# Softmax sums of eight head pairs moved from GpSimd to TensorE, later due times for weight, block and tap writes, and score banks lent to the dense layers, in an attention, gated-convolution and channel-mix kernel

## The chip, the cores and the metric

The program runs on one core of one Trainium2 chip. The time is device microseconds from one launch; lower is better. The core has a matrix engine (TensorE, PE in the rows), three engines for element-wise work (VectorE or DVE, ScalarE or ACT, GpSimd or POOL), and a queue engine (SyncE, SP) that issues all DMAs here. Results of matmuls land in PSUM banks.

## The reference

For 4 batches, 12 heads, 448 rows and 64 columns per head:

```
scores = cap * tanh(q k^T / sqrt(64) / cap)
attn   = exp(scores - max) / (sum(exp(scores - max)) + 1e-9)
x      = attn v, heads side by side: 4 x 448 x 768
gate   = sigmoid(sum over 5 taps of conv_w[k] * x shifted by k rows)
x      = (gate * (x w_val)) w_out
xk, xr = mixtures of x and x shifted by one row, with mu_k and mu_r
out    = sigmoid(xr w_r) * ((max(xk w_k, 0))^2 w_v)
```

q, k and v are 32-bit floats. The weights arrive as 64-bit floats, which the kernel reads as pairs of 32-bit words and narrows itself. w_val, w_out and w_r are 768 x 768, w_k 768 x 1024, w_v 1024 x 768.

## The kernel before, in words

Everything is kept transposed, features on the partitions, 448 rows in the free dimension. Two heads make a pair; there are 24 pairs, six to a batch. A dense product takes each operand as two parts, `hi` (a rounded copy) and `lo` (the rest), and multiplies hi by hi, hi by lo and lo by hi, so one 128 x 128 block costs three matmuls (L644).

**A pair** is six pieces (`piece`, L720). Piece 0: scores of key blocks 0 and 1, tanh on ScalarE (L246), exp on ScalarE (L253), and the first add of the exps on GpSimd (`add_up`, L262). Piece 1: the product with v of the pair before (`pv`, L286), and its copy to `x_f` on ScalarE (L288). Pieces 2 and 3: the transposes of the next pair's q and k on TensorE (L211), split on VectorE (L172, L175) or later ScalarE and VectorE. Piece 4: key blocks 2 and 3, tanh, exp, the other adds (L271, L274). Piece 5: `sums` of the pair before: two matmuls with a block of ones over the added-up exps (L294), which give each row's sum on all 64 partitions of its head. For the last two pairs of a batch VectorE turns the sums into reciprocals at once (L299, L300); for the others the sums go through DRAM and come back as R. `prep` then has GpSimd multiply `x_f` by R (L379), splits it into the block's parts (`x_split`), and adds up the five taps of the gate (L390 on ScalarE for the first, L396 on VectorE for the others). A sigmoid over the whole gate (L400) ends it.

**Order.** The order on every engine is the order of the program text: `in_order` ties each instruction to the one before it on its engine, so an instruction that waits holds all behind it. Work is put later by `post(n, ...)`, which runs it n calls of `step()` from now; a step is one piece, or one half of a dense output.

**Stages.** The first eight pairs (`FIRST`, L20) run by themselves, with the narrowing of the first three w_val blocks between them (L456 to L461). Then the dense layers val and out run batch by batch (`first_stage`), with the rest of the pairs put between their halves at 1.5, 1.5 and 1.35 pieces a half (`behind_first`, L794). In batch 0 each weight block of val and out is narrowed one block ahead and cut into parts by `w_make` (L492): hi on ScalarE, lo on GpSimd or VectorE, the result stored to DRAM for the other batches. The narrowed block lies in one of two buffers (`mk`, L114), so a new block's first step (L456, ScalarE) waits until both halves' lo parts of the block two before are made. With batch 3 the attention is over; w_k and w_v are narrowed into resident tiles while val, out and the second stage (r, k, v; `second_stage`) run. `evac` (L567) takes each dense result out of PSUM; `store` (L612) transposes each output block on TensorE and sends it out.

**PSUM.** `ps_d` has two banks for dense results, `ps_s` two tiles of two banks each for scores, `ps_v` and `ps_m` one each.

The lines that the change touches: `add_up` (L262), `pv` (L276), `sums` (L290), the due times in `prep` (L403 to L412), `x_split` (L426), `w_make` (L492), and the PSUM tile and the place of `store` in `layer` (L625).

Of the kernel before, what the change touches and what calls it, by code (L numbers as in the profile page):

```python
# [46 lines left out]
def attention_gated_conv_channel_mix_kernel(  # L47
# [78 lines left out]
    ones = const.tile([128, 64], F32, name="ones")  # L126
    inv_c = const.tile([128, 1], F32, name="inv_c")
# [13 lines left out]
    def dma(**kw):  # L141
        nc.sync.dma_start(**kw)
# [119 lines left out]
    def add_up(i, n):  # L262

        t = t_t[i]
        eng = nc.gpsimd
        if n == 0:
            acc_t[i] = pools["x"].tile([128, 2, S], F32, tag="acc", name="acc")
            eng.tensor_tensor(acc_t[i], t[:, 0:2], t[:, 2:4], ALU.add)  # L268
            return
        acc = acc_t[i]  # L270
        eng.tensor_tensor(acc, acc, t[:, 4:6], ALU.add)  # L271
        for h in range(2):
            r = slice(64 * h, 64 * h + 64)
            eng.tensor_tensor(acc[r, h], acc[r, h], t[r, 6], ALU.add)  # L274

    def pv(i):  # L276
# [4 lines left out]
        t = t_t.pop(i)  # L281
# [8 lines left out]
    def sums(i):  # L290
        acc = acc_t.pop(i)
        ps = ps_m.tile([128, S], F32, tag="sum", name="sum")
        for h in range(2):
            nc.tensor.matmul(ps[64 * h:64 * h + 64], lhsT=ones, rhs=acc[:, h], start=True, stop=True)  # L294
# [74 lines left out]
    def prep(b, hp, early=False):  # L369
# [39 lines left out]
        for k in range(TAPS):  # L409
            at(4 + (k + 1) // 2 if early else 15 + k, tap, k)  # L410
        if hp == KD - 1:
            at(4 + (TAPS + 1) // 2 if early else 15 + TAPS, sigmoid)  # L412
# [13 lines left out]
    def x_split(b, hp):  # L426
        assert again[0] or b * NP + hp in divided
        x_blk[b, hp] = split_blk(x_f[b * NP + hp], nc.scalar, engines["PD"[hp % 2]], 0 if again[0] else 1)
# [63 lines left out]
    def w_make(nm, o, a, lo_eng):  # L492
# [4 lines left out]
        split_hi(nc.scalar, wp[:, 0], t)  # L497
        post(2 if steps[0] < dense_from[0] else 1, split_lo, lo_eng, wp[:, 1], t, wp[:, 0])
        post(7, lambda: dma(out=parts_d[nm, o][a], in_=wp.bitcast(F32)))
# [122 lines left out]
    n_half = [-1]  # L622
    pend = []

    def layer(b, nm, behind):  # L625
# [4 lines left out]
        for o in range(no):  # L630
            ps = ps_d.tile([128, S], F32, tag="d", name="psd")
            for a in range(2):
# [3 lines left out]
                for kk in range(a * h, a * h + h):  # L636
# [11 lines left out]
                    if kk == 1 and pend:  # L648
                        store(*pend.pop())
# [56 lines left out]
    nc.vector.memset(ones, 1.0)  # L706
    for n in range(2):
        for h in range(2):
            nc.gpsimd.memset(vz[n][h][64 - 64 * h:128 - 64 * h], 0.0)
# [148 lines left out]
    def end_first():  # L858
# [5 lines left out]
        w_resident()  # L864

# [12 lines left out]
    with tc.If(cap_bits > CAP_BITS):  # L878
# [4 lines left out]
        again[0] = True  # L883
        stage.enter_context(first_pools())
# [47 lines left out]
```

## Time and profile before

| | us |
|---|---|
| three runs | 859.79, 860.77, 861.51 (median 860.77) |
| the profiled execution, its own time | 858.22 |
| its span, first to last instruction | 856.4 |
| TensorE busy in the span | 752.1 (88%) |
| VectorE busy | 496.3 (58%) |
| ScalarE busy | 441.9 (52%) |
| GpSimd busy | 344.7 (40%) |
| mean granted TensorE clock, of full speed | 0.952 |

The busy times are of engines that run side by side, so they do not add up to the span, and each is an average over stages with different limits. The row "PEclk" of the profile and of its windows is the granted clock of TensorE as a share of full speed, 2.4 GHz; it has two levels, 2.4 and 1.2 GHz, and a value between is a mean over a stretch. In rows of a timeline the first number is the start, the second the duration in microseconds, and the bracket gives the idle time of the engine before the instruction and what ended it. An "x2" matmul of the program shows as two or four records where the profiler cuts 32-bit matmuls in two, and a few records are missing.

### The profile page before, as it was taken

The numbers are of one execution on the slowest core, as the hardware profiler recorded it, in microseconds if no ns is written. First come the engines' busy times: TensorE is split into PE (matmuls) and PEld (weight loads), VectorE is DVE, ScalarE is ACT, GpSimd is POOL, SyncE is SP. The second block draws the span as 40 slices with busy tenths as digits, with TensorE's granted clock in tenths as the row PEclk, the third lists the DMA queues.
The fourth block names the chain that finished last, engine by engine and source line by source line (L and its number), as shares of the span: only waits on it lengthen the run. The fifth ranks groups of instructions, "written<-read, shape, count | busy, mean of one in ns | idle before, by whom it ended". The sixth has DMA issues, their size and how long they took to land.

```text
span 856.4 us, 10628 instructions
## 1 busy us (share of the span) xinstructions
PE 752.1 (88%) x3798; PEld 578.8 (68%) x3798; DVE 496.3 (58%) x646; ACT 441.9 (52%) x669; POOL 344.7 (40%) x262
## 2 busy tenths in 40 slices
PE   5986678886889798899979887979999999999996
PEld 3433345554556455576668777769999999999996
DVE  5579968968737677654477676885323332333320
ACT  5775566565577566756443465443433353335310
POOL 3787645657535466545716557781000000000000
PEclk8899789988999999999999999999999999999999
DMA  5633316667556677664577996332901380244001
GB/s 140 181 87 99 95 49 192 196 195 220 159 173 203 209 239 230 192 182 134 173 248 242 320 325 227 97 119 73 290 11 43 108 265 1 57 136 149 1 22 47
DMA packets 143931, 131.23 MB, mean 153 GB/s; under 512 B 75767, under 2 KB 123895, under 8 KB 143870
## 3 DMA queue, kind: packets, MB, share of 16 engines
q1 hardware_dynamic: 143870, 130.47, 50.0%
q8 instruction: 32, 0.52, 0.3%
q14 instruction: 29, 0.24, 0.1%
HBM read 105.16 MB, written 25.22 MB: 152 GB/s over the span
## 4 chain that ended last, share of the span: by engine, by line
PE 44%; DVE 23%; ACT 12%; DMA 8%; POOL 7%; issue 5%; SPq 1%; POOLq 0%; ACTq 0%; DVEq 0%
PE psd L644 37%; DVE gate L396 7%; DVE wr L460 3%; PE pv L286 3%; PE s L244 2%; ACT t L253 2%; ACT t L246 2%; DVE wr L459 2%; DMA of<-out 2%; POOL acc L271 2%; DVE wr L461 2%; POOL acc L274 2%; DMA x<-in_moe_w_k_dram 1%; POOL xf L379 1%; ACT t L249 1%
## 5 line engine op out<-in xcount | busy, mean ns | idle before, releaser
L644 PE MATMUL psd<-blk,wp 128*128 128x448 f32 x1296 | 298.5, 383 | 26.1 <-DVE blk L175 9.9
L644 PEld LDWEIGHTS psd<-blk,wp 128*128 128x128 f32 x1296 | 246.5, 196 | 73.5 <-issue 21.5
L644 PE MATMUL psd<-blk,wv 128*128 128x448 f32 x576 | 125.8, 375 | 1.4 <-ACT blk L170 1.1
L644 PE MATMUL psd<-blk,wk 128*128 128x448 f32 x576 | 118.5, 366 | 2.7 <-DVE f L589 2.6
L644 PEld LDWEIGHTS psd<-blk,wk 128*128 128x128 f32 x576 | 107.9, 188 | 12.7 <-DVE f L589 4.2
L644 PEld LDWEIGHTS psd<-blk,wv 128*128 128x128 f32 x576 | 109.0, 192 | 10.8 <-ACT blk L170 1.5
L170 ACT CAST blk<-f 128x448 fp32r<-128x448 f32 x104 | 58.9, 567 | 105.0 <-DVE f L605 51.4
L396 DVE SCALAR_TENSOR_TENSOR gate<-xf,vecT,gate 128x447 f32<-128x447 f32 (+2 forms) x96 | 88.7, 936 | 33.2 <-ACT gate L390 32.3
L175 DVE TENSOR_TENSOR blk<-f,blk 128x448 fp32r<-128x448 f32 x104 | 77.4, 744 | 49.4 <-ACT blk L170 49.4
L271 POOL TENSOR_TENSOR acc<-acc,t 128x896 f32<-128x896 f32 x24 | 52.5, 2189 | 108.3 <-ACT t L253 108.2
L244 PE MATMUL s<-qh,kh 64*128 64x448 f32 x192 | 45.1, 463 | 39.1 <-ACT t L246 24.8
L253 ACT ACTIVATE t<-t 128x1792 f32<-128x1792 f32 (+1 forms) x48 | 72.6, 1512 | 1.5
L246 ACT ACTIVATE t<-s 128x896 f32<-128x896 f32 x72 | 63.7, 915 | 17.3 <-PE s L244 17.2
L286 PE MATMUL pv<-t,vn 128*64 128x448 f32 x288 | 67.1, 606 | 0.0
L274 POOL TENSOR_TENSOR acc<-acc,t 64x448 f32<-64x448 f32 x48 | 62.5, 1303 | 3.6
L268 POOL TENSOR_TENSOR acc<-t 128x896 f32<-128x896 f32 x24 | 54.0, 2248 | 22.5 <-ACT t L253 13.5
L605 DVE SCALAR_TENSOR_TENSOR f<-of,vecT,prev 128x448 f32<-128x448 f32 x48 | 33.5, 698 | 48.0 <-ACT prev L603 48.0
L244 PEld LDWEIGHTS s<-qh,kh 64*128 64x128 f32 x192 | 18.7, 188 | 61.8 <-ACT t L246 35.3
L458 POOL TENSOR_SCALAR wr<-wr 128x384 f32<-128x384 f32 (+1 forms) x28 | 53.8, 1921 | 15.9 <-ACT wr L456 15.8
L589 DVE TENSOR_TENSOR f<-psd,kr 128x448 f32<-128x448 f32 x32 | 19.9, 622 | 61.4 <-ACT kr L587 61.4
L460 DVE SCALAR_TENSOR_TENSOR wr<-x,wr 128x768 int32<-128x768 int32 (+2 forms) x46 | 49.3, 1072 | 1.6
L618 ACT COPY on<-pso 112x512 f32<-112x512 f32 x24 | 14.1, 586 | 68.1 <-PE pso L616 67.8
(81 smaller groups left out, 911.2 us busy)
## 6 DMA issues: line engine op xcount, KB each, us to landing
wp<-pdr SPq DMA_DIRECT2D x48, 384.0 KB
wp<-pdval SPq DMA_DIRECT2D x36, 384.0 KB
wp<-pdout SPq DMA_DIRECT2D x36, 384.0 KB
of<-out SPq DMA_DIRECT2D x48, 224.0 KB
x<-in_moe_w_k_dram SPq DMA_DIRECT2D x16, 384.0 KB
x<-in_moe_w_v_dram SPq DMA_DIRECT2D x12, 512.0 KB
qn<-in_q_dram SPq DMA_DIRECT2D x48, 112.0 KB
kn<-in_k_dram SPq DMA_DIRECT2D x48, 112.0 KB
```

Of the source, the lines that this page charges most:

```text
L170: eng.copy(dst, src)
L175: eng.tensor_tensor(dst, src, hi.bitcast(F32), ALU.subtract)
L244: nc.tensor.matmul(ps[:, h], lhsT=a[r, keys[h]], rhs=x[r], start=(m == 0), stop=(m == 2))
L246: nc.scalar.activation(out=t_t[i][:, at:at + 2], in_=ps, func=ACTF.Tanh, scale=reg_t)
L253: nc.scalar.activation(out=a, in_=a, func=ACTF.Exp, scale=reg_e)
L268: eng.tensor_tensor(acc_t[i], t[:, 0:2], t[:, 2:4], ALU.add)
L271: eng.tensor_tensor(acc, acc, t[:, 4:6], ALU.add)
L274: eng.tensor_tensor(acc[r, h], acc[r, h], t[r, 6], ALU.add)
L286: nc.tensor.matmul(ps[64 * h:64 * h + 64], lhsT=w, rhs=t[:, at], start=(n == 0), stop=(n == 3))
L396: eng.scalar_tensor_tensor(g[:, k:], x[:, :S - k], w, g[:, k:], ALU.mult, ALU.add)
L460: lambda: D.scalar_tensor_tensor(mi, hw, -(1 << 30), mi, ALU.bitwise_and, ALU.bitwise_or),
L644: nc.tensor.matmul(ps, lhsT=lhsT, rhs=x[xp], start=(kk == 0 and m == 0), stop=(kk == kb - 1 and m == 2),)
```

## The change

The exps of the first eight pairs are no longer added up on GpSimd. `add_up` returns at once for them, and `sums` multiplies the seven blocks of exps themselves with ones, and the last block, which holds one head in each half of the partitions, with two new constants that are one in one half and zero in the other. That makes eight matmuls with 32-bit operands in place of two. `t_t` is now given up in `sums`, not in `pv`.

Several writes get later due times. In `w_make` hi goes out one step later, lo after three steps (before: two, and one in the dense stages), the store to DRAM after eight (seven). The lo part of an x block comes two steps behind its hi (one). In `prep` the taps after the first move a step away from it, and the sigmoid with them. From batch 3 on every second dense output takes its PSUM tile from the score pool, which is idle by then, and `store` stands in the second half of an output rather than the first.

```diff
     def add_up(i, n):
+        if i < FIRST:
+            return
@@ pv
-        t = t_t.pop(i)
+        t = t_t[i]
@@ sums
-        acc = acc_t.pop(i)
         ps = ps_m.tile([128, S], F32, tag="sum", name="sum")
-        for h in range(2):
-            nc.tensor.matmul(ps[64 * h:64 * h + 64], lhsT=ones, rhs=acc[:, h], start=True, stop=True)
+        if i < FIRST:
+            t = t_t.pop(i)
+            for n in range(4):
+                for h in range(2):
+                    w, at = (ones, 2 * n + h) if n < 3 else (halves[h], 6)
+                    nc.tensor.matmul(ps[64 * h:64 * h + 64], lhsT=w, rhs=t[:, at], start=(n == 0), stop=(n == 3))
+        else:
+            acc = acc_t.pop(i)
+            for h in range(2):
+                nc.tensor.matmul(ps[64 * h:64 * h + 64], lhsT=ones, rhs=acc[:, h], start=True, stop=True)
@@ prep
-            at(4 + (k + 1) // 2 if early else 15 + k, tap, k)
+            at((5 if k == 0 else 6 + k // 2) if early else 15 + k + (k > 0), tap, k)
         if hp == KD - 1:
-            at(4 + (TAPS + 1) // 2 if early else 15 + TAPS, sigmoid)
+            at(6 + (TAPS + 1) // 2 if early else 16 + TAPS, sigmoid)
@@ x_split
-        ..., 0 if again[0] else 1)
+        ..., 0 if again[0] else 2)
@@ w_make
-        split_hi(nc.scalar, wp[:, 0], t)
-        post(2 if steps[0] < dense_from[0] else 1, split_lo, lo_eng, wp[:, 1], t, wp[:, 0])
-        post(7, lambda: dma(out=parts_d[nm, o][a], in_=wp.bitcast(F32)))
+        post(1, split_hi, nc.scalar, wp[:, 0], t)
+        post(3, split_lo, lo_eng, wp[:, 1], t, wp[:, 0])
+        post(8, lambda: dma(out=parts_d[nm, o][a], in_=wp.bitcast(F32)))
@@ layer
-            ps = ps_d.tile([128, S], F32, tag="d", name="psd")
+            if free_s[0] and o % 2:
+                ps = ps_s.tile([128, 2, 512], F32, tag="s", name="psd")[:, 0, :S]
+            else:
+                ps = ps_d.tile([128, S], F32, tag="d", name="psd")
-                    if kk == 1 and pend:
+                    if kk == h + 1 and pend:
                         store(*pend.pop())
```

`halves` are set by four writes on GpSimd at the start; `free_s` is set when batch 3 begins.

**TensorE, a pair of the first eight.** Before, pieces 2 to 5 and the start of the next pair (psq: a transposed q or k; s: scores; sum: the sums):

```order
L211 MATMUL psq<-ident,qn 128x112 x4
L211 MATMUL psq<-ident,kn 128x112 x4
L244 MATMUL s<-qh,kh 128x448 x2
L244 MATMUL s<-ql,kh 128x448 x2
L244 MATMUL s<-qh,kl 128x448 x2
L244 MATMUL s<-qh,kh 64x448 x2
L244 MATMUL s<-ql,kh 64x448 x2
L244 MATMUL s<-qh,kl 64x448 x2
L294 MATMUL sum<-acc,ones 64x448 x2
```

The same place with the change:

```order
L212 MATMUL psq<-ident,qn 128x112 x4
L212 MATMUL psq<-ident,kn 128x112 x4
L245 MATMUL s<-qh,kh 128x448 x2
L245 MATMUL s<-ql,kh 128x448 x2
L245 MATMUL s<-qh,kl 128x448 x2
L245 MATMUL s<-qh,kh 64x448 x2
L245 MATMUL s<-ql,kh 64x448 x2
L245 MATMUL s<-qh,kl 64x448 x2
L300 MATMUL sum<-t,ones 64x448 x6
L300 MATMUL sum<-t,half_91 64x448
L300 MATMUL sum<-t,half_92 64x448
```

Two matmuls became eight; nothing else moved on TensorE here.

**ScalarE, where the first dense layer begins.** Before (t: the exps, first tanh then exp; gate: the sigmoid of batch 0; wr: a narrowed weight block; wp: its parts):

```order
L253 ACTIVATE t<-t 128x1344
L306 COPY rows<-sum 128x448
L400 ACT_TABLE_LOAD
L400 ACTIVATE gate<-gate 128x2688
L246 ACTIVATE t<-s 128x896 x2
L253 ACT_TABLE_LOAD
L253 ACTIVATE t<-t 128x1792
L456 ACTIVATE wr<-x_1055 128x768
L170 CAST wp<-wr 128x384
```

With the change:

```order
L254 ACTIVATE t<-t 128x1344
L316 COPY rows<-sum 128x448
L247 ACTIVATE t<-s 128x896 x2
L254 ACTIVATE t<-t 128x1792
L466 ACTIVATE wr<-x_1060 128x768
L410 ACT_TABLE_LOAD
L410 ACTIVATE gate<-gate 128x2688
L171 CAST wp<-wr 128x384
```

The sigmoid and its table load stand behind the next pair's tanh and exp and behind the first step of a weight block.

**GpSimd, a pair in the dense stages of batch 0.** Before (acc: the added-up exps; wp: the lo part of a weight; xf: the multiplication by R; vz: the padded v):

```order
L271 TENSOR_TENSOR acc_1092<-acc_1092,t_1067 128x896
L274 TENSOR_TENSOR acc_1092<-acc_1092,t_1067 64x448 x2
L175 TENSOR_TENSOR wp_1220<-wr_1086,wp_1220 128x384
L379 TENSOR_TENSOR xf_980<-xf_980,R_1203 128x448
L268 TENSOR_TENSOR acc_1263<-t_1237 128x896
```

With the change:

```order
L274 TENSOR_TENSOR acc_1099<-acc_1099,t_1072 128x896
L277 TENSOR_TENSOR acc_1099<-acc_1099,t_1072 64x448 x2
L389 TENSOR_TENSOR xf_985<-xf_985,R_1210 128x448
L176 TENSOR_TENSOR wp_1234<-wr_1093,wp_1234 128x384
L271 TENSOR_TENSOR acc_1276<-t_1250 128x896
```

The lo part of the weight changed places with the multiplication by R.

## Rows read from the trace of the kernel before

**Rows 1.** Windows: stretch, length, busy of PE, PEld, DVE, ACT, POOL, clock, DMA share, GB/s

```profile
57.00:115.00 58.00, 36.91 (x203) 18.84 (x202) 55.61 (x56) 35.09 (x48) 42.35 (x32) 0.86 0.37 100
115.00:257.00 142.00, 117.68 (x598) 75.05 (x599) 99.04 (x120) 94.06 (x135) 76.67 (x59) 0.93 0.55 173
...
430.00:600.00 170.00, 145.07 (x656) 125.82 (x655) 123.02 (x167) 77.53 (x139) 92.09 (x58) 0.95 0.64 208
600.00:857.00 257.00, 249.58 (x1266) 230.40 (x1264) 79.89 (x127) 88.69 (x148) 0.00 (x0) 0.99 0.31 94
```

**Rows 2.** Waits of PE, 0 to 115 us: total us, times, longest

```profile
PE s L244 <- DVE kh L172: 9.4, 4, 3.2
...
PE psd L644 <- DVE blk L175: 4.7, 1, 4.7
...
PE psd L644 <- DVE ql L175: 2.9, 1, 2.9
```

**Rows 3.** Groups of DVE, 57 to 115 us: count, busy us, mean ns, idle before

```profile
L396 DVE SCALAR_TENSOR_TENSOR gate<-xf,vecT,gate 128x447 f32<-128x447 f32 (+3 forms) x24 | 26.7, 1135 | 1.8 <-ACT gate L390 1.6
...
L461 DVE SCALAR_TENSOR_TENSOR wr<-x,wr 128x768 int32<-128x768 int32 x1 | 2.9, 2910 | 0.0
...
L460 DVE SCALAR_TENSOR_TENSOR wr<-x,wr 128x768 int32<-128x768 int32 x1 | 2.6, 2611 | 0.0
```

**Rows 4.** The taps (tile gate) on DVE, 57 to 115 us: ns shortest, median, longest

```profile
L396 DVE SCALAR_TENSOR_TENSOR gate<-xf,vecT,gate x24: 668/716/2512, 59.5 to 114.1; 128x447 f32<-128x447 f32 x6, 128x446 f32<-128x446 f32 x6, 128x445 f32<-128x445 f32 x6, 128x444 f32<-128x444 f32 x6
```

**Rows 5.** Timeline of DVE at 127 us, while POOL is idle

```profile
127.16 0.96 DVE L460 SCALAR_TENSOR_TENSOR wr<-x,wr 128x768 int32<-128x768 int32 x1
128.15 0.96 DVE L461 SCALAR_TENSOR_TENSOR wr<-x,wr 128x768 int32<-128x768 int32 x1
```

**Rows 6.** Groups of POOL, 57 to 115 us

```profile
L274 POOL TENSOR_TENSOR acc<-acc,t 64x448 f32<-64x448 f32 x8 | 11.5, 1441 | 0.6
L268 POOL TENSOR_TENSOR acc<-t 128x896 f32<-128x896 f32 x4 | 8.9, 2219 | 1.6 <-ACT t L253 1.6
L271 POOL TENSOR_TENSOR acc<-acc,t 128x896 f32<-128x896 f32 x4 | 8.6, 2144 | 7.3 <-ACT t L253 7.3
```

**Rows 7.** Timeline of PE, pairs 3 and 6

```profile
41.16 2.48 PE L286 MATMUL pv<-t,vn 128*64 128x448 f32 x12
43.47 0.92 PE L286 MATMUL pv<-t,vz 128*64 128x448 f32 x4
...
46.65 0.97 PE L294 MATMUL sum<-acc,ones 128*64 128x448 f32 x4
49.69 0.47 PE L244 MATMUL s<-qh,kh 64*128 64x448 f32 x2 [2.07 <-DVE kh L172]
...
84.87 1.74 PE L294 MATMUL sum<-acc,ones 128*64 128x448 f32 x4 [2.61 <-DVE R L299]
```

**Rows 8.** Timeline of POOL and of ACT at 160 us

```profile
160.26 1.51 POOL L379 TENSOR_TENSOR xf<-xf,R 128x448 f32<-128x448 f32 x1
...
160.33 0.90 ACT L456 ACTIVATE wr<-x 128x768 f32<-128x768 f32 x1 [3.49 <-POOL wp L175]
```

**Rows 9.** Waits of PE, 115 to 257 us

```profile
PE psq L211 <- ACT xf L288: 13.1, 6, 5.6
PE s L244 <- ACT t L246: 10.1, 6, 4.1
```

**Rows 10.** Waits of PE, 430 to 520 us and 520 to 600 us

```profile
PE psd L644 <- ACT f L576: 2.0, 3, 1.2
PE psd L644 <- DVE f L572: 1.5, 1, 1.5
...
PE psd L644 <- ACT r L581: 3.6, 1, 3.6
PE psd L644 <- DVE f L589: 2.6, 3, 0.9
PE pso L616 <- DVE oT L593: 2.3, 1, 2.3
```

More of the change, by code (lines that the diff above doesn't have):

```diff
@@ L126, in attention_gated_conv_channel_mix_kernel @@
     ones = const.tile([128, 64], F32, name="ones")
+    halves = [const.tile([128, 64], F32, name=f"half{h}") for h in range(2)]
     inv_c = const.tile([128, 1], F32, name="inv_c")
@@ L427, in x_split @@
         assert again[0] or b * NP + hp in divided
-        x_blk[b, hp] = split_blk(x_f[b * NP + hp], nc.scalar, engines["PD"[hp % 2]], 0 if again[0] else 1)
+        x_blk[b, hp] = split_blk(x_f[b * NP + hp], nc.scalar, engines["PD"[hp % 2]], 0 if again[0] else 2)
     layers = {"val": (w_val, KD, KD), "out": (w_out, KD, KD), "r": (w_r, KD, KD), "k": (w_k, KD, KF), "v": (w_v, KF, KD)}
@@ L622, in attention_gated_conv_channel_mix_kernel @@
     n_half = [-1]
+    free_s = [False]
     pend = []
@@ L706, in attention_gated_conv_channel_mix_kernel @@
     nc.vector.memset(ones, 1.0)
+    for h in range(2):
+        nc.gpsimd.memset(halves[h], 0.0)
+        nc.gpsimd.memset(halves[h][64 * h:64 * h + 64], 1.0)
     for n in range(2):
@@ L864, in end_first @@
         w_resident()
+        free_s[0] = True
     for b in range(B):
@@ L883, in attention_gated_conv_channel_mix_kernel @@
         again[0] = True
+        free_s[0] = False
         stage.enter_context(first_pools())
```

## The prediction

> **What bounds the kernel now.** I read the windows first, because the shares of the whole span mix stages. From 600 us on TensorE is busy for 249.6 of 257 us at a clock of 0.99 [rows 1]: nothing that another engine gives up can shorten that part. From 57 to 115 us, the last half of the eight lone pairs and the start of the dense layers, TensorE is busy for only 36.9 of 58 us, at a clock of 0.86, while VectorE is busy for 55.6: VectorE sets the pace there. From 115 to 257 us no engine is full (TensorE 117.7 of 142), and from 430 to 600 TensorE is busy for 145.1 of 170; there it is waits between queues that run in program order.
>
> Then I read what TensorE waits for up to 115 us [rows 2]: 9.4 us for VectorE's split of k, 4.7 for a block's lo part and 2.9 for a split of q, all VectorE's work. So VectorE's queue is behind. Why, the groups of VectorE say [rows 3]: 24 taps took 26.7 us, 1.135 us each, though the shortest took 0.668 [rows 4]. One L460 took 2.61 us and one L461 2.91; the same two took 0.96 each at 127 us, with GpSimd idle [rows 5]. In the slow stretch GpSimd was busy for 42.4 us. Something that GpSimd does holds VectorE up, and 11.5 + 8.9 + 8.6 = 29.0 us of GpSimd's 42.4 are the adds of the exps [rows 6], which the change takes away.
>
> **The change, part by part.**
>
> *Sums on TensorE, its own cost.* The product with v is also eight 32-bit matmuls of 64 columns and 448 rows. In pair 3 it ran from 41.16 to 43.47 + 0.92 = 44.39 us, 3.23 us; the two matmuls of the sums took 0.97 [rows 7]. So each of the eight pairs costs TensorE 3.23 - 0.97 = 2.26 us more, 18 us in all. At the lower clock it would be more: the two matmuls took 1.74 us at 84.87 us, 1.8 times as long.
>
> *What VectorE gets back, 57 to 115 us.* Taps: 26.7 - 24 x 0.668 = 10.7 us over their shortest. L460 and L461: 2.6 + 2.9 - 2 x 0.96 = 3.6. Together 14.3. The adds are 29.0 / 42.4 = 68% of GpSimd's time, so I give them 68% of it, 9.8 us; the rest stays with the multiplications, the padding of v and the blocks' parts, which remain on GpSimd. VectorE then needs 55.6 - 9.8 = 45.8 us; 41.3 if all of it were the adds'.
>
> *What TensorE needs in the same stretch.* 36.9 + 4 x 2.26 = 45.9 us at the clock it had. If the clock were full throughout, about 0.86 x 36.9 + 9.0 = 40.8. In these rows the clock falls after TensorE has idled: the sums at 84.87 us, behind an idle 2.61 us, ran 1.8 times as long as those at 46.65. The longer sums stand just where TensorE waited for the next k, so they fill that wait and the clock should stay up for most of it. I take 45 us for the stretch in place of 58, between the 41 of both engines at their best and the 48 that they would take with a wait or two left over: **-13 us**. Behind it the first dense products no longer wait for a block (4.7) and the sigmoid no longer stands ahead of the next pair's tanh on ScalarE; both are inside the 58 us.
>
> *Before 57 us.* Three pairs carry longer sums there, 3 x 2.26 = 6.8 us, and of the waits for k one of 2.07 us, at 49.69, stands behind a sum there [rows 7]; the two longest come ahead of any sum. **+4.5 us**. The eighth pair's sums fall into the dense stage, where they add 2.26 to TensorE; that is covered by TensorE's 24 idle us between 115 and 257. The four writes to the new constants run on GpSimd in the first microseconds, while all wait for the first DMA: nothing.
>
> The Trainium skill, page "SBUF — State Buffer", section "SBUF: two separate sides", says that VectorE and GpSimd share a pair of ports under an exclusive lock, and that whoever loses it blocks for the other's whole instruction. Rows 3 to 5 agree in direction; by the lock VectorE could get back up to all 14.3 us, the stretch would then be bounded by TensorE at 41 to 46 us, and the sum below would change by 4 us at most.
>
> *Later due times.* In batch 0 the lo part of the second half of a weight block moves behind the multiplication by R on GpSimd. ScalarE's first step on a later block waits for that lo part, 3.49 us at 160.33, and the multiplication that now comes ahead takes 1.51 us [rows 8]. Behind that ScalarE step stands the copy of `x_f`, for which TensorE waits 13.1 us in six places between 115 and 257 [rows 9]. Four weight blocks stand so: 4 x 1.5 = +6 us at worst, and R might not have landed by then. On the other side lo and the taps no longer stand ahead of the dense results on VectorE, hi no longer ahead of a block's hi on ScalarE, and the 10.1 us that TensorE waits for tanh [rows 9] are partly ScalarE standing behind them: down to -10 at best. I take **0** between +6 and -10, since the block that waits and the work that waits behind it both have rows of the same size. The stores to DRAM one step later are read a batch later: nothing, as the loads of batch 1 are issued far behind them.
>
> *Score banks for the dense layers, and the later transposes.* Between 430 and 600 us TensorE waits for a dense result to leave PSUM 2.0 + 1.5 + 3.6 + 2.6 = 9.7 us [rows 10]. With four banks in place of two TensorE can run two outputs further before it waits. But ScalarE and VectorE there also narrow the resident weights, in program order, and VectorE is busy for 123 of 170 us: what TensorE gains it partly waits for at the next layer's first blocks. Ends 0 and -9.7; I take **-5**. The transposes waited 2.3 us for VectorE's last product [rows 10]; half an output later they need not: **-1**. Behind 600 us there are 7 us of idle TensorE in all, and I count nothing there.
>
> The Trainium skill, page "TensorE: Matmul & The Clock Gate", section "HAM oscillation — how this bites in real kernels", reports a matmul kernel to which double-buffering of PSUM gave no further gain. By that the 5 us would be 0 and the forecast 5 us later; no wait for a bank is told of there, and rows 10 show four kinds of them here.
>
> **Sum.** -13 + 4.5 + 0 - 5 - 1 = -14.5 us against the profiled execution: 858.2 - 14.5 = 843.7. The median of the runs is 860.77, 2.6 above that execution; carried over the forecast is **846 us**.
>
> **Rivals.**
>
> *A. All of it pays.* VectorE gets back all 14.3 us and TensorE's clock stays up: 41.3 us in the stretch (-17), +3 before it, -8 from the later due times, -8 from the banks: -30, **831 us**. For it: the waits exist and each has its row. Against: waits that are taken away one by one seldom add up, because the queue behind is late too.
>
> *B. Nothing is left over.* The lone pairs gain 8 us as forecast, the weights' lo parts behind the multiplications give 6 back in batch 0, and the banks bring nothing since the narrowing of the resident weights sets the pace from 430 to 580 us: -2, **859 us**, within 856 and 862.
>
> *C. Slower: TensorE becomes the bound in the lone pairs.* The sums put 18 us on TensorE's queue, on the path in every pair, if the waits for VectorE come from the order of its queue rather than from GpSimd. Then VectorE is still as late, TensorE waits behind its longer sums, and only the waits for k, some 4 us, are covered: +14, less 4 for the banks: +10, **871 us**. It decides from the point at which 57 to 115 us shrinks by less than the 4.5 us that the first pairs lose. Against it: rows 3 to 5, the same instruction at 0.96 and at 2.9 us.
>
> *D. The change does less than it says.* TensorE no longer waits for a bank but waits as long for the next layer's blocks, because ScalarE and VectorE write them between the narrowing steps at the same pace as before. That is the forecast without its -5 and -1, **852 us**. For it: VectorE's 123 of 170 us [rows 1]; against: 3.6 us of the waits are a single one, at a copy of r, where all blocks of the layer are there. The Trainium skill's report on double-buffered PSUM, named above, is of this kind.
>
> **How the numbers follow.** The forecast 0.45 (838 to 850 us), D 0.12, A 0.20, B 0.11, C 0.12. 846 is the likeliest. The range of 831 to 862 us leaves out C and the far end of A. About 0.2%, 1.7 us, is what a measurement of this kernel can tell from no change. Faster: the forecast, D, A and half of B, 0.82. Same: the other half of B, 0.06. Slower: C, 0.12.
>
> **What would show each step.** Sums of about 3.2 us on TensorE in each lone pair, at the full clock; GpSimd nearly idle up to 100 us; taps of 0.67 to 0.8 us and L460 and L461 near 0.96 there; the work of 57 to 115 us done in some 45. In batch 0, ScalarE's L456 waiting for GpSimd for 3 to 5 us where it was 3.5, or not, tells the term that I set to zero. From 430 to 600 us no more waits of TensorE for the copies out of PSUM, and the question whether waits for blocks grew in their place. The forecast is wrong if the taps stay above 1 us without the adds, if the clock in the lone pairs stays at 0.86, or if TensorE's idle time from 115 to 257 us grows by more than the first stage gains.

## The result, and the profile after

| | before | after |
|---|---|---|
| median of four runs each, us | 860.28 | 844.90 |
| all runs, us | 859.79 to 861.51 | 842.49 to 846.59 |
| the profiled execution, its own time, us | 858.22 | 846.59 |
| its span, us | 856.4 | 844.7 |
| TensorE's mean granted clock | 0.952 | 0.957 |

The ratio is 0.9833, with a 95% interval of 0.9805 to 0.986: faster by 1.7%. The forecast was 846 us.

The windows of the kernel after, columns as in [rows 1]. The stages begin some 15 us earlier, so the stretches are set to the same work:

```profile
57.00:100.00 43.00, 41.08 (x258) 21.14 (x255) 38.27 (x52) 34.94 (x48) 12.81 (x14) 1.00 0.45 118
100.00:240.00 140.00, 117.43 (x608) 75.96 (x607) 100.65 (x125) 92.72 (x133) 74.76 (x59) 0.93 0.59 181
415.00:585.00 170.00, 147.07 (x666) 128.28 (x665) 122.88 (x168) 78.49 (x143) 95.42 (x61) 0.93 0.63 208
585.00:845.00 260.00, 252.03 (x1280) 232.68 (x1278) 79.55 (x128) 89.90 (x150) 0.00 (x0) 0.99 0.31 94
```

Only the first line is another picture: TensorE is busy for 41.1 of 43 us at a clock of 1.00, where it had 36.9 of 58 at 0.86. The other three look as before.

The groups of VectorE, then of GpSimd, 57 to 115 us of the kernel after, to be read against [rows 3, 6] (L406 is the old L396; L470 and L471 the old L460 and L461; L271, the first add, the old L268):

```profile
L406 DVE SCALAR_TENSOR_TENSOR gate<-xf,vecT,gate 128x447 f32<-128x447 f32 (+3 forms) x24 | 19.1, 822 | 0.1
...
L470 DVE SCALAR_TENSOR_TENSOR wr<-x,wr 128x768 int32<-128x768 int32 x2 | 2.6, 1304 | 0.0
...
L471 DVE SCALAR_TENSOR_TENSOR wr<-x,wr 128x768 int32<-128x768 int32 x2 | 1.9, 954 | 0.0
```

```profile
L389 POOL TENSOR_TENSOR xf<-xf,R 128x448 f32<-128x448 f32 x5 | 6.7, 1345 | 22.7 <-DMA R<-recd 14.4 <-DVE R L310 8.4
...
L271 POOL TENSOR_TENSOR acc<-t 128x896 f32<-128x896 f32 x1 | 2.4, 2427 | 7.4 <-ACT t L254 7.4
```

The same 24 taps take 19.1 us in place of 26.7, and two of each narrowing step take 4.5 us where one of each took 5.5. Of the adds only the one of the ninth pair is left.

TensorE in a lone pair of the kernel after, from its timeline, to be read against [rows 7]:

```profile
49.76 2.48 PE L300 MATMUL sum<-t,ones 128*64 128x448 f32 x12
52.06 0.92 PE L300 MATMUL sum<-t,half 128*64 128x448 f32 x4
...
59.84 2.48 PE L300 MATMUL sum<-t,ones 128*64 128x448 f32 x12
62.15 0.92 PE L300 MATMUL sum<-t,half 128*64 128x448 f32 x4
```

The sums take 62.15 + 0.92 - 59.84 = 3.23 us, as forecast to the hundredth, and a pair goes by every 10.1 us.

Where the time went along the run is seen best from marks on TensorE that every kernel has: the start of the product with v of a pair (pair 7 ends the lone pairs, 18 and 19 lie on both sides of batch 1's sigmoid), the first matmul with w_k and with w_v (both of batch 0), and with w_v in batch 1. All from the timelines, in us; the last six columns are experiments told below:

| mark | before | after | sums_only | no_banks | store7 | lo_back | weights_back | combined |
|---|---|---|---|---|---|---|---|---|
| pair 3 | 51.6 | 54.3 | 54.4 | 53.3 | 53.2 | 52.1 | 53.8 | 52.0 |
| pair 7 | 115.3 | 102.0 | 102.2 | 101.0 | 101.0 | 99.9 | 101.7 | 99.8 |
| pair 18 | 338.5 | 324.2 | 325.2 | 322.0 | 319.1 | 315.1 | 314.0 | 316.8 |
| pair 19 | 359.1 | 349.2 | 348.2 | 347.9 | 343.3 | 341.5 | 340.4 | 338.8 |
| w_k, batch 0 | 525.8 | 511.6 | 512.7 | 515.8 | 502.4 | 502.0 | 502.5 | 503.2 |
| w_v, batch 0 | 559.0 | 540.9 | 547.3 | 549.2 | 532.1 | 531.4 | 533.0 | 532.3 |
| w_v, batch 1 | 651.7 | 639.1 | 639.9 | 641.1 | 629.3 | 629.8 | 629.6 | 630.6 |

Each column is one execution, which can lie some us off its kernel's median (of the traces used below, no_sums 5.8 and adds_kept 5.1 above it, store7 2.7 below). Over the traces of all kernels the product with v of pair 0 starts at 18.3 to 21.2 us, which shifts a whole column. Kernels whose code is the same up to pair 23 differ as well: from pair 7 to pair 23 after takes 309.2 us, no_banks 308.8 and store_back 307.9, but sums_only 308.0 and sums_banks 303.2. So a difference of under some 5 us between two columns, taken alone, need not come from the edit.

The kernel after is 13.3 us ahead at pair 7, 14.3 at pair 18, only 9.9 at pair 19, 18.1 at w_v of batch 0, and 12.6 at w_v of batch 1. So nearly all of the gain is made in the lone pairs; two later pieces make and lose 4 to 6 us.

### The profile page after: what moved, and what is told of

The parts are those of the page before. It is cut to its first block, busy times and chain, and to the rows that moved or that the text cites. A ratio compares the mean times of both kernels' runs of the same rounds, so it can differ in the third digit from the quotient of the medians.

```text
span 844.7 us, 10769 instructions
## 1 busy us (share of the span) xinstructions
PE 759.2 (90%) x3894; PEld 585.8 (69%) x3894; DVE 463.5 (55%) x646; ACT 441.9 (52%) x669; POOL 283.6 (34%) x234
## 4 chain that ended last, share of the span: by engine, by line
PE 53%; DVE 18%; DMA 10%; ACT 9%; issue 5%; POOL 4%; SPq 1%; ACTq 0%; POOLq 0%; DVEq 0%
PE psd L659 40%; PE pv L289 5%; DVE gate L406 4%; PE s L245 4%; DVE wr L470 3%; DMA of<-out 2%; DVE wr L469 2%; DMA pdr<-wp 2%; DVE wr L471 2%; PE sum L300 2%; DVE R L310 1%; ACT t L247 1%; DMA rec<-rows 1%; PE pso L626 1%; SPq L143 1%
## 5 line engine op out<-in xcount | busy, mean ns | idle before, releaser
L659 PEld LDWEIGHTS psd<-blk,wp 128*128 128x128 f32 x1296 | 247.4, 196 | 65.8 <-issue 20.6
L659 PE MATMUL psd<-blk,wv 128*128 128x448 f32 x576 | 127.6, 377 | 6.7 <-ACT blk L171 4.2
L406 DVE SCALAR_TENSOR_TENSOR gate<-xf,vecT,gate 128x447 f32<-128x447 f32 (+3 forms) x96 | 78.2, 830 | 17.7 <-ACT gate L400 16.9
L274 POOL TENSOR_TENSOR acc<-acc,t 128x896 f32<-128x896 f32 x16 | 35.0, 2191 | 84.2 <-ACT t L254 84.2
L289 PE MATMUL pv<-t,vn 128*64 128x448 f32 x288 | 60.8, 558 | 0.0
L599 DVE TENSOR_TENSOR f<-psd,kr 128x448 f32<-128x448 f32 x32 | 19.9, 622 | 62.0 <-ACT kr L597 62.0
L603 DVE TENSOR_TENSOR oT<-psd,r 128x448 f32<-128x448 f32 x24 | 15.0, 623 | 70.8 <-PE psd L659 70.8
L466 ACT ACTIVATE wr<-x 128x768 f32<-128x768 f32 (+2 forms) x46 | 33.2, 721 | 30.4 <-POOL wp L176 20.9
L470 DVE SCALAR_TENSOR_TENSOR wr<-x,wr 128x768 int32<-128x768 int32 (+2 forms) x46 | 45.9, 997 | 1.5
L389 POOL TENSOR_TENSOR xf<-xf,R 128x448 f32<-128x448 f32 x24 | 30.9, 1291 | 46.6 <-DMA R<-recd 28.1
## 6 DMA issues: line engine op xcount, KB each, us to landing
of<-out SPq DMA_DIRECT2D x48, 224.0 KB
```

Of the source, the lines that this page charges most:

```text
L289: nc.tensor.matmul(ps[64 * h:64 * h + 64], lhsT=w, rhs=t[:, at], start=(n == 0), stop=(n == 3))
L406: eng.scalar_tensor_tensor(g[:, k:], x[:, :S - k], w, g[:, k:], ALU.mult, ALU.add)
L470: lambda: D.scalar_tensor_tensor(mi, hw, -(1 << 30), mi, ALU.bitwise_and, ALU.bitwise_or),
L659: nc.tensor.matmul(ps, lhsT=lhsT, rhs=x[xp], start=(kk == 0 and m == 0), stop=(kk == kb - 1 and m == 2),)
```

## Experiments

The theory was that GpSimd's adds of the exps hold up VectorE (and through it TensorE and its clock), so that taking them away is what pays; that the later due times are worth about nothing; and that the score banks pay some 5 us. The rivals: the longer sums keep TensorE busy and its clock up, so that they and not the adds are the gain; or the due times or the banks carry it. Each run's ratio is to the kernel before on the same chip (its median was 858.84 us for no_sums, adds_kept, sums_only and no_banks, 858.53 for taps_back, taps_batch0, weights_back and store_back, 857.38 for the last four). Times of kernels of different groups are compared by their ratios.

### Sums and adds: no_sums, adds_kept, sums_only

**no_sums**: the change without its first part.

```diff
     def add_up(i, n):
-        if i < FIRST:
-            return
@@ pv
-        t = t_t[i]
+        t = t_t.pop(i)
@@ sums
-        if i < FIRST:
+        if i < 0:
```

> The changed kernel with the exps of the first eight pairs added up on GpSimd again and two matmuls for the sums; all later due times and the score banks stay. Theory (the adds on GpSimd slow VectorE, which sets the pace of the lone pairs): the taps of 57 to 115 us take over 1 us each again, the product with v of pair 7 starts 10 to 13 us later than 102, and the time is 855 to 858 us. Rival (the lone pairs gain because the taps, the blocks' lo parts and the sigmoid come later): pair 7 starts within 3 us of 102 and the time is 845 to 848.

Measured: 854.28 us, ratio 0.9942 (0.992 to 0.9964).

**adds_kept**: TensorE makes the sums as in after, but GpSimd still adds up the exps of the first eight pairs; that result is not read.

```diff
     def add_up(i, n):
-        if i < FIRST:
-            return
```

> The changed kernel, sums on TensorE, but GpSimd still does all the adds of the first eight pairs, whose result nobody reads. Theory (the adds slow VectorE): pair 7's product with v starts 10 us or more later than 102, GpSimd's adds and VectorE's taps both stretch, 855 to 862 us. Rival 1 (the longer sums help by themselves, since they keep TensorE busy and its clock up): within 2 us of the changed kernel, 843 to 847. Rival 2 (the gain was that TensorE need not wait for GpSimd's last add): also 843 to 847.

Measured: 858.53 us, ratio 1.0001 (0.9987 to 1.0015).

**sums_only**: the kernel before with the sums on TensorE and nothing else of the change.

> The kernel before with the sums of the first eight pairs on TensorE and nothing else. Theory: most of the gain of the lone pairs is this edit alone; pair 7's product with v starts at 103 to 106 us, 848 to 851 us. Rival (without the later due times the sigmoid and the blocks still hold the queues where the dense layers begin): pair 7 at 108 or later, 854 to 858.

Measured: 845.99 us, ratio 0.9846 (0.9789 to 0.9904). This one and no_sums came out 2.0 and 0.7 us below the times expected. No_sums also shows that the rest of the change, without its first part, is 5 us faster than the kernel before; beside the moved sums no such gain can be told, since sums_only and after have the same ratio within their intervals.

The window of 57 to 100 us, of no_sums, of adds_kept and of sums_only, columns as above:

```profile
57.00:100.00 43.00, 29.50 (x156) 13.88 (x156) 42.05 (x38) 27.59 (x36) 32.25 (x26) 0.80 0.36 92
```

```profile
57.00:100.00 43.00, 37.44 (x217) 16.74 (x214) 39.32 (x39) 30.00 (x39) 32.29 (x26) 0.92 0.34 88
```

```profile
57.00:100.00 43.00, 41.67 (x259) 21.27 (x256) 38.14 (x53) 33.92 (x47) 12.80 (x14) 1.00 0.45 117
```

VectorE is busy for 38 to 42 of the 43 us in all three, but it gets through 38, 39 and 53 instructions. So with the adds it is not idle, waiting for GpSimd's other results; its own instructions take longer. The taps there (shortest, median and longest, in ns), first adds_kept, then sums_only:

```profile
L404 DVE SCALAR_TENSOR_TENSOR gate<-xf,vecT,gate x24: 582/808/2553, 63.9 to 118.8; 128x447 f32<-128x447 f32 x6, 128x446 f32<-128x446 f32 x6, 128x445 f32<-128x445 f32 x6, 128x444 f32<-128x444 f32 x6
```

```profile
L406 DVE SCALAR_TENSOR_TENSOR gate<-xf,vecT,gate x24: 631/678/1567, 59.8 to 101.5; 128x447 f32<-128x447 f32 x6, 128x446 f32<-128x446 f32 x6, 128x445 f32<-128x445 f32 x6, 128x444 f32<-128x444 f32 x6
```

How a single one is held up stands in adds_kept's timelines of VectorE and of GpSimd (L404 is a tap, L469 the last narrowing step, before's L461):

```profile
77.77 2.54 DVE L404 SCALAR_TENSOR_TENSOR gate<-xf,vecT,gate 128x447 f32<-128x447 f32 x1
...
84.40 2.89 DVE L469 SCALAR_TENSOR_TENSOR wr<-x,wr 128x768 int32<-128x768 int32 x1
```

```profile
77.72 2.11 POOL L272 TENSOR_TENSOR acc<-acc,t 128x896 f32<-128x896 f32 x1 [1.51 <-ACT t L254]
...
83.97 2.51 POOL L269 TENSOR_TENSOR acc<-t 128x896 f32<-128x896 f32 x1
```

The add runs from 77.72 to 79.83; the tap that begins 0.05 us behind it ends at 80.31, 0.48 us after the add, no more than a tap's own time. The narrowing step of 84.40 ends 0.81 us after the add that began ahead of it at 83.97, and alone it takes 0.96 [rows 5]. So a VectorE instruction of this kind that begins during an add waits the add out. The same holds for all: 9 of the 24 taps of adds_kept begin during an add, and each of the 9 ends 0.48 us after that add, whether the add began 0.05 or 1.94 us before the tap. That is what the Trainium skill says, page "SBUF — State Buffer", section "SBUF: two separate sides": where a VectorE instruction has two inputs in SBUF, as these have, the port pair that the two engines share goes to whoever starts first, for its whole instruction, and the other one stands still; the rows here agree.

And in adds_kept the sums themselves, on TensorE's timeline:

```profile
73.25 2.48 PE L298 MATMUL sum<-t,ones 128*64 128x448 f32 x12
...
88.54 4.75 PE L298 MATMUL sum<-t,ones 128*64 128x448 f32 x12 [4.93 <-DVE R L307]
```

After an idle 4.93 us they ran at the lower of the two clocks, 1.2 GHz (granted clock 0.50 from 88 to 94 us), for nearly twice as long. The clock in the stretch was 0.92, with the longer sums in place; so they don't keep it up by themselves. What follows: with the adds still there the sums on TensorE cost 118.1 - 112.4 = 5.7 us up to pair 7 (adds_kept against no_sums), and taking the adds away then gives 118.1 - 102.0 = 16.1. By the ratios of the whole times it is 5 and 14 us (0.9942 to 1.0001, and 1.0001 to 0.9833). The rival falls. The lone part of the change, sums_only, has the whole 13 us, and its total cannot be told from that of after. In all eleven traced kernels without these adds pair 3 to pair 7 takes 47.6 to 47.9 us; in the three with them, before, no_sums and adds_kept, it takes 60.4 to 63.7.

### The score banks and the transposes: no_banks, store_back

**no_banks**: after with all dense results in their two own banks.

```diff
-        free_s[0] = True
+        free_s[0] = False
```

> The changed kernel with dense results in the two banks of before; the rest stays. Theory (the banks gain 8 us up to the v layer of batch 0 and lose most of it there to waits for blocks): 846 to 849, the first product with w_v some 4 to 8 us later than 540.9, the second stage of batch 1 only 2 to 4 us later. Rival (all 8 us are kept): 852 to 854. Rival (banks bring nothing): 844 to 846.

Measured: 846.97 us, ratio 0.9851 (0.9814 to 0.9887); after has 0.9833 (0.9805 to 0.986). What TensorE waits for from 500 to 585 us (total, times, longest), of no_banks, then of after:

```profile
PE psd L659 <- ACT r L591: 4.7, 2, 3.5
PE pso L626 <- ACT on L628: 4.0, 1, 4.0
PE psd L659 <- DVE f L599: 2.8, 3, 0.9
PE psd L659 <- ACT blk L171: 1.1, 1, 1.1
...
```

```profile
PE psd L659 <- ACT blk L171: 4.2, 2, 3.7
PE pso L626 <- ACT on L628: 2.8, 1, 2.8
PE psd L659 <- DVE blk L176: 2.5, 2, 2.3
PE psd L659 <- DMA wp<-pdr: 2.5, 1, 2.5
```

With four banks no wait for the copies out of PSUM (L591, L599) is left. At w_v of batch 0 after stands 8.3 us ahead of no_banks; then it waits 2.3 and 3.7 us for the blocks of that layer, and in batch 1 it is 2.0 ahead. Counted from pair 23, up to which the code is the same, that is 9.7 us and 3.4 us. The three traced kernels with two banks (before, sums_only, no_banks) take 229.8 to 231.3 us from pair 23 to w_v of batch 1, the eleven with four 224.1 to 229.7, 227.2 in the mean: some 3 us are kept. One reason stands on VectorE's timeline of after:

```profile
549.97 0.98 DVE L470 SCALAR_TENSOR_TENSOR wr<-x,wr 128x512 int32<-128x512 int32 x1
550.98 0.69 DVE L471 SCALAR_TENSOR_TENSOR wr<-x,wr 128x512 int32<-128x512 int32 x1
551.59 0.62 DVE L599 TENSOR_TENSOR f<-psd,kr 128x448 f32<-128x448 f32 x1
```

The product f (L599), from which the block for w_v is cut, stands behind the narrowing of a piece of w_v, in program order. TensorE comes earlier and waits for it. Rival D of the prediction is what happened to 6 of these 9 us; some 3 stay, which the times cannot tell from nothing.

**store_back**: after with the transposes in the first half of the next output again.

```diff
-                    if kk == h + 1 and pend:
+                    if kk == 1 and pend:
```

> The changed kernel with the transposes of the output back in the first half of the next dense output. Theory (they are hidden by the other waits of the v layer of batch 0, and at the very end the later place costs about 1 us, because the last two output blocks leave closer together): 843 to 845, 0 to 1.5 us faster. Rival (each transpose waits for VectorE's product, 2 to 4 us in all): 846 to 849.

Measured: 843.14 us, ratio 0.9827 (0.98 to 0.9854): no difference from after that these intervals can tell.

### The due times: taps_back, taps_batch0, weights_back

**taps_back**: taps, sigmoid and the lo parts of the x blocks are due as before.

```diff
-            at((5 if k == 0 else 6 + k // 2) if early else 15 + k + (k > 0), tap, k)
+            at(4 + (k + 1) // 2 if early else 15 + k, tap, k)
-            at(6 + (TAPS + 1) // 2 if early else 16 + TAPS, sigmoid)
+            at(4 + (TAPS + 1) // 2 if early else 15 + TAPS, sigmoid)
@@ x_split
-        ..., 0 if again[0] else 2)
+        ..., 0 if again[0] else 1)
```

> The changed kernel with the taps, the sigmoid and the lo parts of the x blocks due as before; sums on TensorE, weight due times and score banks stay. Theory (the later taps gain some 3.5 us where the first dense layer begins, because the sigmoid no longer holds ScalarE, and lose 3 to 4 us at 336 to 344, where the sigmoid of batch 1 stands in front of a pair's tanh and comes later): the two cancel, 843 to 847; the product with v of pair 8 starts 2 to 4 us later than 119.8, that of pair 19 within 2 us of 349.2. Rival (the later taps are a clear gain): 848 to 852. Rival (a clear loss): 839 to 842.

Measured: 843.34 us, ratio 0.9843 (0.9815 to 0.987).

**taps_batch0**: these later due times for batch 0 alone (the same lines, chosen by `b`).

> The changed kernel with the later taps, sigmoid and lo parts in batch 0 alone; batches 1 to 3 have the due times of before. Theory: the gain at the first dense layer stays (pair 8 at 119.8) and the loss of 3 to 4 us at the sigmoid of batch 1 goes (pair 19 at 345 to 346): 840 to 843. Rival (the wait for tanh there has another cause, such as the narrowing of w_r on VectorE): pair 19 at 348 to 350, 843 to 847.

Measured: 841.94 us, ratio 0.9809 (0.9782 to 0.9836).

Neither can be told from after by its time, but the marks show two effects of opposite sign. At pair 8, behind batch 0's sigmoid, after stands at 119.8 us and taps_back at 123.7, though taps_back was 2 us ahead at pair 7; taps_batch0 has 119.8 as well. Without the adds of the first pairs, pair 7 to pair 8 takes 17.8 or 17.9 us in all eight kernels with the later taps of batch 0, and 21.1 to 23.8 in the three without. At batch 1's sigmoid after loses. VectorE, ScalarE and TensorE, from the timelines of after:

```profile
335.51 0.96 DVE L471 SCALAR_TENSOR_TENSOR wr<-x,wr 128x768 int32<-128x768 int32 x1
336.39 2.11 DVE L406 SCALAR_TENSOR_TENSOR gate<-xf,vecT,gate 128x446 f32<-128x446 f32 x3
```

```profile
338.57 1.28 ACT L410 ACT_TABLE_LOAD   x1 [6.97 <-DVE gate L406]
...
343.04 0.92 ACT L247 ACTIVATE t<-s 128x896 f32<-128x896 f32 x1
```

```profile
344.01 0.74 PE L245 MATMUL s<-qh,kh 64*128 64x448 f32 x2 [7.61 <-ACT t L247]
```

The last three taps came later on VectorE, behind the narrowing of a piece of w_r, so the sigmoid waited for them for 7.0 us, and the next tanh stood behind the sigmoid. With the taps as before (taps_back) this wait of TensorE is 2.8 us. Pair 18 to pair 19 takes 24.2 to 26.4 us in the eight traced kernels with the later taps of batch 1, and 20.6 to 23.0 in the six without. In taps_batch0 pair 19 starts at 347.1 us, later than the 345 to 346 expected, but its wait is 2.7 us as well.

**weights_back**: the parts of the dense weights and their store are due as before.

```diff
-        post(1, split_hi, nc.scalar, wp[:, 0], t)
-        post(3, split_lo, lo_eng, wp[:, 1], t, wp[:, 0])
-        post(8, lambda: dma(out=parts_d[nm, o][a], in_=wp.bitcast(F32)))
+        split_hi(nc.scalar, wp[:, 0], t)
+        post(2 if steps[0] < dense_from[0] else 1, split_lo, lo_eng, wp[:, 1], t, wp[:, 0])
+        post(7, lambda: dma(out=parts_d[nm, o][a], in_=wp.bitcast(F32)))
```

> The changed kernel with the weights' hi, lo and store due as before. Theory (a wash, as forecast: what lo gives up behind the multiplication by R it gets back on VectorE): 843 to 847, pair 13 within 2 us of 229.2. Rival (the later lo parts cost: ScalarE waits 20.9 us for them from 104 to 240): 839 to 842, pair 13 at 223 to 226. Rival (they gain): 848 or more, pair 13 at 233 or later.

Measured: 837.74 us, ratio 0.9764 (0.9742 to 0.9786): faster than after, the intervals do not meet. I had expected a wash; it is below even the rival's 839 to 842, whose mechanism it shows, with pair 13 at 224.0 us. ScalarE's waits in after, 104 to 240 us, and 240 to 330 us:

```profile
ACT wr L466 <- POOL wp L176: 20.9, 7, 7.1
```

```profile
ACT wp L171 <- DMA pdr<-wp: 21.1, 4, 6.5
```

With the weights as before they are 8.7 and 5.4 us. The first is the wait of a narrowing step for the lo part two blocks back; the second that of a new hi part for a buffer whose store to DRAM has not landed.

### Which half of the weights: store7, lo_back

**store7**: after with `post(8, ...)` of the store set to `post(7, ...)`, nothing else.

> After, with one number changed: the store of a dense weight's parts is due seven steps behind w_make, as before, in place of eight; the parts themselves stay late (hi one step, lo three steps behind). Theory S (the store holds the ring of six weight buffers, so that ACT's next hi part waits for it: 21.1 us of that wait between 240 and 330 us in after against 5.4 with the weights as before): nearly the whole gain of the weights put back is here, 838 to 840 us, the wait of wp for the store between 240 and 330 us falls to under 10 us, and the product with v of pair 18 starts 6 us or more earlier than after's 324.2. Rival L (lo behind the multiplication by R on GpSimd is what costs, since ACT's narrowing steps wait for it: 20.9 us in after against 8.7): 843 to 846 us, and ACT's wait of wr for GpSimd's lo between 104 and 240 us stays near 20 us.

Measured: 839.69 us, ratio 0.9786 (0.9756 to 0.9816).

**lo_back**: hi and lo as in weights_back, the store at eight steps as in after.

> The other half of the same split: hi and lo of a dense weight are written as early as before, lo ahead of the multiplication by R on GpSimd again, and the store stays at eight steps. Theory S: 843 to 846 us, the wait of wp for the store between 240 and 330 us stays near 20 us. Rival L: 838 to 840 us, the wait of wr for lo between 104 and 240 us falls to about 9 us. If both carry a part, each kernel lands near 841 us.

Measured: 838.33 us, ratio 0.9773 (0.9745 to 0.98).

In store7 the wait for the store fell to 5.0 us and that for the lo part stayed, and the time is that of theory S. Pair 18 starts 5.1 us earlier, not 6, and 4.1 of these are gained behind pair 7. ScalarE's waits of store7, 104 to 240 and 240 to 330 us:

```profile
ACT wr L466 <- POOL wp L176: 19.4, 7, 6.8
```

```profile
ACT wp L171 <- DVE wr L471: 11.6, 3, 5.0
ACT wp L171 <- DMA pdr<-wp: 5.0, 1, 5.0
```

The same of lo_back:

```profile
ACT wp L171 <- DVE wr L471: 19.5, 8, 5.5
ACT wr L466 <- POOL wp L176: 10.3, 7, 2.1
```

```profile
ACT wp L171 <- DVE wr L471: 21.6, 5, 5.4
```

The wait for the lo part fell to 10.3 us, as rival L said. But in the second stretch no wait for the store is left at all, with the store at eight steps still, where theory S said some 20 us. In its place the hi parts, written earlier, wait 21.6 us for the narrowing. (For the store and the narrowing together they wait 27.8 us there in after, 16.6 in store7 and 21.6 in lo_back.) So the wait for the store also goes when only the parts are written earlier; why was not traced.

I expected the halves to share some 7 us. By the ratios store7 gave 4.0 us against after, lo_back 5.2 and both together 5.9; the interval of store7 still meets that of after (0.9816 and 0.9805), and with some 3 us to either side of each figure the times don't show whether the halves add up. In the traces they nearly do up to pair 18: counted from pair 7, after takes 222.2 us, store7 218.1, lo_back 215.2, weights_back 212.3, that is 4.1, 7.0 and 9.9 us less. Behind it the sums meet other limits: at batch 1's sigmoid TensorE waits 8.0 us in lo_back and weights_back and 6.1 in store7, and at w_v of batch 1 all three stand within 0.5 us of each other. That store7 makes up 3 us on weights_back between pair 23 and w_k is not explained: there weights_back waits 3.1 us for parts of w_r read back from DRAM and store7 2.3. These 3 us may be of the one execution that was traced, which lies 2.7 us below the median of store7.

What the lo part does is seen at one block, on GpSimd and then on ScalarE. In after:

```profile
165.77 1.15 POOL L389 TENSOR_TENSOR xf<-xf,R 128x448 f32<-128x448 f32 x1
166.88 1.02 POOL L176 TENSOR_TENSOR wp<-wr,wp 128x384 fp32r<-128x384 f32 x1
```

```profile
167.93 0.90 ACT L466 ACTIVATE wr<-x 128x768 f32<-128x768 f32 x1 [3.68 <-POOL wp L176]
...
169.56 0.53 ACT L291 COPY xf<-pv 128x448 f32<-128x448 f32 x1
```

In lo_back:

```profile
163.10 1.00 POOL L176 TENSOR_TENSOR wp<-wr,wp 128x384 fp32r<-128x384 f32 x1
164.06 1.15 POOL L389 TENSOR_TENSOR xf<-xf,R 128x448 f32<-128x448 f32 x1
```

```profile
164.14 0.92 ACT L466 ACTIVATE wr<-x 128x768 f32<-128x768 f32 x1 [2.12 <-POOL wp L176]
...
165.79 0.54 ACT L291 COPY xf<-pv 128x448 f32<-128x448 f32 x1
```

The wait is 1.56 us shorter, with the multiplication of 1.15 us no longer ahead, and the copy of `x_f` behind it, for which TensorE waits, comes earlier too: by 3.77 us, of which 2.1 are lo_back's lead at pair 7. (Lo_back also writes the hi part a step earlier; no run has the lo part alone.) From 104 to 240 us TensorE waits for that copy 15.4 us in after and 6.0 in lo_back. Not all of this is gain: its waits for tanh, which stands in the same queue, rise from 4.3 to 12.3 us there, and from pair 7 to pair 13 lo_back is 3.7 us quicker (123.5 us against 127.2).

### What is left: combined, sums_banks

**combined**: the sums, the banks, the later taps of batch 0; weights, transposes and batch 1 as before. **sums_banks**: the same without the later taps, sigmoid and blocks' lo parts.

> Sums on TensorE and the score banks for dense outputs as in after, the later due times of taps, sigmoid and blocks' lo in batch 0 alone, weights' parts and store as before, transposes as before. The three pieces that were undone one by one gave 7.2, 3.0 and 1.8 us below after's 844.9 each; if they added up it would be 833 us. Since the weights put back already take the batch 1 stall at the sigmoid from its place, I expect 834 to 838 us, no slower than the weights put back alone (837.7).

Measured: 838.79 us, ratio 0.9776 (0.9744 to 0.9809).

> Before plus two parts of the change: the sums on TensorE and the score banks; all due times and the transposes as before. Against the combined kernel it lacks only the later taps, sigmoid and blocks' lo in batch 0. Against the sums alone (846.0) it adds only the banks. Theory that the banks are worth what the trace showed at the first v layer and lose it again by batch 1: 843 to 845 us. Rival, that they keep it when the weights' parts and store are early, so that the work behind them is ready: 837 to 840 us. If the later taps of batch 0 are worth the 3.5 us that they gained at the first dense layer, this one is 2 to 4 us above the combined kernel.

Measured: 843.90 us, ratio 0.9838 (0.9809 to 0.9867).

Combined is no better than weights_back, and above the 834 to 838 us expected. The gains of 7.2, 3.0 and 1.8 us that were added up for it are 5.9, 2.1 and 0.5 by the ratios, and only the first is clear of the intervals. Beside the earlier taps of batch 1 the weights' part is also worth less: combined has 0.9776 where taps_batch0 has 0.9809, 2.8 us, with intervals that overlap. Its wait at batch 1's sigmoid is 2.7 us in place of 8.0, but from pair 7 to pair 18 it takes 217.0 us in place of 212.3, about what it wins at the sigmoid; why was not traced. Sums_banks differs from it in the later due times of batch 0 alone: they are worth 5.1 us here, with intervals that touch at 0.9809 only. And sums_banks against sums_only (0.9838 and 0.9846) shows nothing for the banks by the times, with the weights early, and 1.3 us from pair 23 to w_v of batch 1: the rival that they would keep their whole gain falls.

The fastest version that ran is weights_back, the change without its `w_make` part, 837.7 us: 2.4% below the kernel before, and by the two ratios 0.7% below the kernel after. The ratios of lo_back, combined and store7 cannot be told from its own.

## Why the prediction was right

**Sums on TensorE**: 3.23 us forecast, 3.23 measured. Right.

**VectorE gets back 9.8 us**: the taps gave 26.7 - 19.1 = 7.6 and L460 and L461, 5.5 us for one of each, cost (2.6 + 1.9) / 2 = 2.3, 3.2 less: 10.8 us. Right, and adds_kept shows that it is the adds.

**The lone pairs, -13 + 4.5 = -8.5 us**: measured -13.3 at pair 7. Mechanism right, both terms mis-sized. Up to pair 3 the change lost 2.7 us in place of 4.5, and 1.0 of them stand at the product with v of pair 0 already, ahead of any sum. From pair 3 to pair 7 it took 47.7 us in place of 63.7, -16.0 in place of -13. The term that was mis-sized is the choice of 45 us "in place of 58, between the 41 of both engines at their best and the 48": 58 - 16 is 42, and in after TensorE is busy for 41.1 of the 43 us from 57 to 100 at the full clock. What it still waits for up to 115 us in after (total, times, longest), against [rows 2]:

```profile
PE s L245 <- DVE kh L173: 6.3, 2, 4.0
...
PE psd L659 <- DVE ql L176: 1.5, 1, 1.5
...
PE psd L659 <- DVE blk L176: 0.8, 1, 0.8
```

Both waits for k end before 19 us, ahead of any sum; the two behind a sum, 2.07 us at 49.69 and 2.12 at 61.47 before, are gone. (In [rows 2] the two ahead of any sum are 3.24 and 1.97 us, the longest and the shortest, not the two longest; the sum does not rest on it.) So rival A was nearly right for this stage, in its 41.3 us and its clock, though VectorE got back 10.8 us and not 14.3.

**Later due times, 0 between +6 and -10**: as a whole sums_only and after cannot be told apart, and neither can taps_back and after; but the zero is a difference of larger terms. From pair 7 to pair 23 after took 309.2 us where before took 305.7, so by the marks they cost some 3 us, no more than the spread of such marks. The weights' parts and store cost about 6 us (0.9833 - 0.9764 = 0.0069 of 860). The lo part behind the multiplication, which I had as the bad end, did cost what its row said, 1.56 us at the block shown, and lo_back gave back 5.2 us where the bad end was 6. The sentence on the stores, "read a batch later: nothing", asked who reads the stored parts and not what the store holds: it holds a buffer for which ScalarE waited 21.1 us in after and 5.0 in store7. That this costs time is likely but not shown, 4.0 us by ratios whose intervals meet. The later taps of batch 0 give up to 5 back, and those of batch 1 lose some 4 at the sigmoid, a loss that I had not looked for.

**Score banks, -5**: some 3 us by the marks from pair 23 on, between the 0 and the 5, and not more than the times can tell from nothing. Rival D, 0.12, was right that the next layer's blocks take most of it back. **Transposes, -1**: not shown. From 500 to 585 us TensorE waits ahead of a transpose for 2.8 us in after, 3.0 with the transposes put back (store_back), and 4.2 us in before, where [rows 10] has only the 2.3 of them.

**Sum**: -14.5 forecast, -15.4 between the medians. The large term and its cause were right; that the total is so close is in part luck. By the marks the lone pairs gave 5 us more than I took, and against that the banks gave 2 less, the transposes nothing that shows, and the due times cost some 3. The profiled executions, from which the marks are, differ by 11.6 us only.

**Rival C** fell, since VectorE was late because of GpSimd and not of its own order; adds_kept shows what C would have looked like, some 5 us lost against no_sums.

## What to carry to other kernels

When one engine's instruction takes 1 us here and 2.9 us there, look at what the other engine runs at that moment, and move that work to an engine with idle time, even where it costs more there: 18 us more of matmuls over eight pairs took the place of 57 us of adds and bought 13 us of span. For every write that is put later, ask which buffer it now holds longer and who waits for that buffer, a store to DRAM as much as a product; and read the wait again after each edit, since here it moved from the store to the narrowing. And undo the parts of a mixed change one by one: here one of its parts cost 6 us, and without it the kernel is faster. Trace kernels that share their code up to some point, too: how far their marks differ there is what a single trace cannot tell.

## What the runs showed of the hardware

- An add on GpSimd does not slow a tap or a narrowing step on VectorE by a share; it holds it until the add is over: in adds_kept a tap took 2.54 us beside an add of 2.11 us and 0.58 to 0.68 without, and all 9 taps that began during an add ended 0.48 us after it. From 57 to 115 us VectorE lost some 11 us to 29 us of adds, so not every add meets such an instruction.
- TensorE's granted clock: with the longer sums but late inputs it was 0.92 from 57 to 100 us, without them 0.80, and with inputs in time 1.00. Behind an idle 4.93 us the sums took 4.75 us at 1.2 GHz in place of 2.48 at 2.4.
- A buffer stays taken until its store to DRAM has landed: ScalarE's hi parts waited 21.1 us for such stores in after from 240 to 330 us, and 5.0 with the store issued one step earlier (store7).
- A wait can change its place: in lo_back, 5 us faster than after, no wait for the store is left, but the hi parts wait 21.6 us for the narrowing. Up to pair 18 the two halves of the weights' part gained 4.1 and 7.0 us, and both 9.9.
